# Sink-window attention with a Fourier mix: x transposes ahead of the probabilities' transposes, and three DVE instructions one step later

## The chip, the cores and the metric

The kernel runs on one core of one Trainium2 chip. The metric is the device time of one execution in microseconds (us); lower is better. The engines of the core are named as in the profile: PE is TensorE (PEld its weight loads), DVE is VectorE, ACT is ScalarE, POOL is GpSimd, SP is SyncE, which issues most DMAs.

## The reference

Attention over 4 batches, 8 heads, 768 positions and head width 64, where each query sees the first 4 keys (the sink) and the 128 latest; then a 2-D Fourier transform of the result, of which the real part is added; then a normalization and a two-layer network.

```python
keep = is_sink | in_window            # pos < 4, or 0 <= pos_q - pos_k < 128
a = exp(where(keep, q @ k.T / 8, -1e9) - max)
x = (a / (sum(a) + 1e-9)) @ v         # (4, 8, 768, 64) -> (4, 768, 512)
u = x + real(fft(fft(x, axis=1), axis=2))
un = (u - mean(u)) / sqrt(var(u) + 1e-6)
out = u + max(un @ w_ch1, 0) @ w_ch2  # 512 -> 2048 -> 512
```

## The kernel before, in words

**Groups and steps.** A group g (0 to 23) is one block of 128 queries of one batch, with all 8 heads; six groups make a batch. A step s = 4g + k treats the head pair k of group g. At each step every engine gets its share of several groups, since each operation has a lag in steps: in `STEP_LAG` for operations of a head pair, in `BLOCK_AT` for operations of a whole group.

**One group's path.** Scores s (PE, L703); the newer keys merged in (DVE, L709) and mask with maximum (DVE, L721, called soft1); the exponential (ACT, L727); the transposes of four heads' probabilities into the PSUM tile pt (PE, L755), copied to SBUF as pta (ACT, L762); selects on POOL that make ptl and zero a part of pta (L771, L779); the products with v into xt (PE, L793), copied as xs (ACT, L798); four transposes of xs into x (PE, L805) and one product that adds the sink's share (L807). The sink's probabilities go through a transpose of their own, pk (PE, L811), copied as skt (ACT, L816). POOL adds 1e-9 to the sums (floor, L747), DVE inverts them (inverse, L743) and multiplies x by them into u (store_x, L821).

**The Fourier mix** starts for a batch when its fourth block of u is stored. Stage 1 (L395) makes five PSUM tiles in turn: za0, za1, zr, zb0, zb1. Each is rounded to a high half by ACT (L402, L400 for zr), and DVE subtracts that for the low half (L410, L407 for zr). Stage 2 makes dc and a (L422) and b (L443) for three column blocks; ACT copies a to asb (L431), DVE forms sum and difference (L448, L449; L457 puts in the constant row), and POOL adds them to u (L459, L460). Batches 0 to 2 have stage 1 within attention; batch 3, the tail, has it after attention, beside the network.

**What shares a PSUM bank.** pt and pk have one buffer together. x has one. Stage-1 and stage-2 tiles have the buffer "fft", and at steps with k = 2 (`X_AT`) outside of steps 81 to 97 (`X_NOT`) they take x's buffer: za1 and zb0 of batches 0 and 1 share x's bank, while all five z tiles of batch 2 follow each other in the one "fft" bank. The transposes unx (L545) of the normalized batch 0, read by DVE at L554, share x's bank as well. A PE write to a bank waits for the last read of what was there.

**What sets the order.** Up to step 96 the instructions stand on each engine in the order in which they are recorded, and each engine works through its own queue in order. The table `SCHEDULE` has two phases, of which the second counts from step 36 (`PHASE`); for each engine and each k it lists operations and events: A, G and T are the transform's events on ACT, POOL and PE, and 0 to 3 and V those on DVE. From step 97 (`CUT`) to the end a scheduler orders the instructions. The network is ch1 (L620), relu (L1114, L1119) and ch2 (L1126); its weights are unpacked by DVE (L591 to L593), rounded by ACT (L608), and POOL takes the remainder (L609).

Of the kernel before, what the change touches and what calls it, by code (L numbers as in the profile page):

```python
# [72 lines left out]
    "copy_sink": 10,  # L73
    "sink_hi": 0,
    "floor": 6,
    "inverse": 8,
    "store_x": 13,
    "sink_lo": 2,
    "trans_sink": 9,
# [48 lines left out]
            ["sink_p", "newer_p", "older_p", "G"],  # L128
        ],
        "T": [  # L130
            ["av", "trans_p", "trans_sink", "T", "turn_x"],
            ["T", "trans_sink"],
            ["av", "T", "trans_p", "trans_sink", "turn_x"],
            ["trans_p", "T", "av", "trans_sink", "turn_x"],
# [4 lines left out]
EV_D, EV_Z = 1, 1  # L139
# [67 lines left out]
def kernel(  # L207
# [15 lines left out]
    V, A, G, T = nc.vector, nc.scalar, nc.gpsimd, nc.tensor  # L223

    def f32(ap):
        return ap.bitcast(F32)
# [44 lines left out]
    def run(general):  # L271
        tag = "g" if general else ""
        with ExitStack() as p1:
# [8 lines left out]
            def at(s, eng, fn):  # L282
                ev.setdefault((s, eng), []).append(fn)
# [49 lines left out]
            def fourier(b, at, ready):  # L333
# [49 lines left out]
                def stage1(kind, mc, part, parts):  # L383
                    ps = t_[f"z{kind}{mc}"] if part else psum(f"z{kind}{mc}")
                    ch, cl = (C_hi, C_lo) if kind != "b" else (S_hi, S_lo)
                    lo_c = {"a": P * mc, "r": 256, "b": 257 if mc == 0 else 384}[kind]
                    cs = slice(lo_c, lo_c + P)
                    mm = []
                    for j in range(NHALF):
                        mm += [(gh[:, j, cs], ch[:, j]), (gh[:, j, cs], cl[:, j]), (gl[:, j, cs], ch[:, j])]  # L390
                    if kind != "b":
                        mm += [(sph[:, cs], sgn)]
                    for i, (a, c) in enumerate(mm):
                        if i * parts // len(mm) == part:
                            T.matmul(ps[:, :NK], a, c, start=i == 0, stop=i == len(mm) - 1)  # L395

                def z_hi(kind, mc):
                    ps = t_[f"z{kind}{mc}"]
                    if kind == "r":
                        A.copy(zr[0:1], ps[0:1, :NK])  # L400
                    else:
                        A.copy((za if kind == "a" else zb)[0][:, mc], ps[:, :NK])  # L402

                def z_lo(kind, mc):
                    ps = t_.pop(f"z{kind}{mc}")
                    if kind == "r":
                        V.tensor_tensor(zr[NR - 1:NR], ps[0:1, :NK], f32(zr[0:1]), op=ALU.subtract)  # L407
                    else:
                        z = za if kind == "a" else zb
                        V.tensor_tensor(z[1][:, mc], ps[:, :NK], f32(z[0][:, mc]), op=ALU.subtract)  # L410
# [53 lines left out]
                tail = b == B - 1 or general  # L464
                at(1, "S", load_row)
                for j in range(NHALF):
                    k = ready[j]
# [11 lines left out]
                k = ready[2] + S1  # L479
                n1, na, nb = PARTS_TAIL if tail else PARTS[b]  # L480
                for i, (kind, mc) in enumerate((("a", 0), ("a", 1), ("r", 0), ("b", 0), ("b", 1))):
                    n = n1[i]
                    for part in range(n):
                        at(k + part, "T", lambda kind=kind, mc=mc, part=part, n=n: stage1(kind, mc, part, n))
                    k += n
                    at(k, "A", lambda kind=kind, mc=mc: z_hi(kind, mc))
                    at(k, EV_Z, lambda kind=kind, mc=mc: z_lo(kind, mc))
                k += S2
                for part in range(na):
                    at(k + part, "T", lambda part=part: stage2a(0, "dc", part, na))  # L490
# [143 lines left out]
            hp = []  # L634

            def window_attention(fourier, load_constants):
                with ExitStack() as pa:
                    kpool = pa.enter_context(tc.tile_pool(name="kpool", bufs=1, side="right"))
# [190 lines left out]
                    with ExitStack() as man:  # L829
# [130 lines left out]
                        while s < last:  # L960
# [25 lines left out]
                            for e in "AVGT":  # L986
                                for op in SCHEDULE[s >= PHASE][e][k]:
                                    if op in EVENTS:
                                        if (s, op) == (4, "G"):
                                            load_constants()  # L990
                                        run_ev(s, op)
                                    elif op in STEP_LAG:
                                        lag(table[op], s, STEP_LAG[op])
                                    else:
                                        at_ = s - BLOCK_AT[op]
                                        if at_ % NP == 0 and 0 <= at_ // NP < NQ:
                                            table[op](at_ // NP)
                                            if op == "store_x" and at_ // NP % NB == 3:
                                                b = at_ // NP // NB
                                                fourier(b, lambda d, e, f, s=s: at(s + d, e, f), FOLD_AT if b < B - 1 else FOLD_LAST)  # L1000
                            s += 1
                    extra.clear()
                return last

            def general_attention(fourier):
                for b in range(B):
                    u = uview(b)
# [331 lines left out]
```

## Time and profile before

| | us |
|---|---|
| median of 3 runs | 782.7 (782.69 to 784.17) |
| profiled execution | 786.08 |
| its span | 784.1 |
| mean granted PE clock | 0.991 |
| DVE, ACT, POOL busy | 453.5, 237.1, 185.1 |

Read as follows: the attention with the Fourier mix of batches 0 to 2 fills the first 200 us or so, the mix of batch 3 and the first of the seven groups of the network run up to about 280, and the rest is the network. Step 36 begins near 62 us and step 97 near 199 us of the span. In a row of a timeline stand the start, the duration, the engine, the line, the operation, out<-in and the shape; in brackets the idle time of the engine before it and what ended it. In a row of waits stand the waiting instruction, what it waited for, and the total in us, the count and the longest.

### The profile page before, as it was taken

To read this page: it belongs to the slowest core of one execution; us is meant where nothing else is said; L and a number is where in the kernel's file an instruction comes from. 1 tells how busy PE (TensorE), PEld (TensorE's weight loads), DVE (VectorE), ACT (ScalarE), POOL (GpSimd) and SP (SyncE) were. 2 spreads that over 40 slices of the span, in tenths; PEclk is the share of its full clock that TensorE was granted. 3 is DMA by queue.
4 is the path that set the end of the run, shared out by engine and by line. 5 is a ranking of instruction groups with operands and counts; after the bars stand their busy time and mean duration, and the time that the engine had idled before them with its cause. 6 is when DMAs were issued, how large, how long until landed. Compare 5 with 4: busy or idle time off the path is not lost.

```text
span 784.1 us, 11917 instructions
## 1 busy us (share of the span) xinstructions
PE 755.7 (96%) x4379; PEld 616.8 (79%) x4379; DVE 453.5 (58%) x1330; ACT 237.1 (30%) x704; POOL 185.1 (24%) x307
## 2 busy tenths in 40 slices
PE   7999998989998999999999999999999999999996
PEld 5676876867777878899888888888888888888895
DVE  6878587999999489561456424661456424611211
ACT  4887765766523123221111101111111111110110
POOL 2567477477654255100000000000000000000000
PEclk9999999999999899999999999999999999999998
DMA  9863535434215266110100002000200001000100
GB/s 283 268 177 105 151 83 177 127 112 145 86 50 166 92 196 208 66 59 1 54 0 1 1 18 89 1 0 1 81 0 1 2 1 54 1 0 1 54 1 31
DMA packets 41810, 57.67 MB, mean 74 GB/s; under 512 B 2796, under 2 KB 27500, under 8 KB 41360
## 3 DMA queue, kind: packets, MB, share of 16 engines
q1 hardware_dynamic: 41456, 53.07, 21.6%
q0 software_dynamic: 288, 3.76, 1.3%
q8 instruction: 36, 0.59, 0.3%
q14 instruction: 30, 0.25, 0.1%
HBM read 47.37 MB, written 9.45 MB: 72 GB/s over the span
## 4 chain that ended last, share of the span: by engine, by line
PE 80%; DVE 9%; POOL 4%; issue 3%; ACT 2%; DMA 2%; SPq 1%; POOLq 0%; DVEq 0%; ACTq 0%
PE o L1126 33%; PE h L620 33%; PE s L703 3%; PE xt L793 3%; PE pt L755 2%; PE za L395 1%; DVE cv L592 1%; DVE cv L593 1%; DVE sm L721 1%; PE zb L395 1%; ACT pta L762 1%; ACT sm L727 1%; DMA vt<-in_v_sink_dram 1%; POOL ptl L771 1%; DVE s L709 1%
## 5 line engine op out<-in xcount | busy, mean ns | idle before, releaser
L1126 PE MATMUL o<-w,h 128*128 128x512 f32 x876 | 218.6, 397 | 0.0
L1119 DVE SCALAR_TENSOR_TENSOR h<-h,h 128x512 fp32r<-128x512 f32 (+1 forms) x107 | 65.4, 611 | 250.5 <-ACT h L1114 250.3
L1126 PEld LDWEIGHTS o<-w,h 128*128 128x128 f32 x876 | 164.5, 190 | 36.0
L1114 ACT ACTIVATE h<-h 128x512 fp32r<-128x512 f32 (+1 forms) x107 | 57.1, 534 | 368.6 <-PE h L620 362.4
L620 PE MATMUL h<-un_slots,w 128*128 128x512 f32 (+1 forms) x576 | 124.7, 365 | 0.0
L620 PEld LDWEIGHTS h<-un_slots,w 128*128 128x128 f32 x576 | 99.6, 188 | 19.6
L620 PE MATMUL h<-un_last,w 128*128 128x512 f32 (+1 forms) x432 | 89.0, 355 | 0.0
L620 PEld LDWEIGHTS h<-un_last,w 128*128 128x128 f32 x432 | 72.7, 188 | 12.8
L727 ACT ACTIVATE sm<-sm,mx 128x132 f32<-128x132 f32 x192 | 76.0, 400 | 6.0 <-DVE mx L721 6.0
L1150 DVE STREAM_TRANSPOSE unf<-un 32x128 f32<-32x128 f32 x224 | 67.7, 302 | 3.2
L703 PE MATMUL s<-ring,q 64*128 64x260 f32 x320 | 49.9, 418 | 8.9 <-DVE mx L721 5.3
L721 DVE CUSTOM_DVE_ANT_0 sm<-s,mask 128x132 f32<-128x132 f32 x192 | 48.5, 293 | 6.3 <-PE s L701 1.3
L703 PEld LDWEIGHTS s<-ring,q 64*128 64x128 f32 x320 | 27.3, 188 | 21.6 <-issue 8.0
L609 POOL TENSOR_TENSOR w<-cv,w 128x512 fp32r<-128x512 f32 x25 | 34.1, 1366 | 30.5 <-ACT w L608 30.5
L793 PE MATMUL xt<-ptl,ldv 128*64 128x128 f32 x384 | 39.3, 285 | 0.2 <-POOL ptl L771 0.2
L727 ACT ACTIVATION_READ_ACCUMULATOR sm<-sm,mx 128x1 f32 x192 | 36.7, 191 | 0.0
L1126 PE MATMUL o<-w_ring,h 128*128 128x512 f32 x144 | 35.6, 393 | 0.0
L762 ACT COPY pta<-pt 128x512 f32<-128x512 f32 x48 | 28.0, 583 | 24.9 <-PE pt L755 23.5
L709 DVE COPY_PREDICATED s<-older,s 128x256 f32<-128x256 uint8 x80 | 33.7, 421 | 1.6 <-PE s L703 1.6
L771 POOL TENSOR_SCALAR_AFFINE_SELECT ptl<-pta 128x512 f32<-128x512 f32 x48 | 32.5, 678 | 7.3 <-ACT pta L762 7.2
L793 PEld LDWEIGHTS xt<-ptl,ldv 128*64 128x64 f32 x384 | 21.9, 136 | 15.1 <-issue 6.2
L793 PE MATMUL xt<-pta,ldv 128*64 128x128 f32 x320 | 31.7, 274 | 0.3 <-POOL pta L779 0.3
(197 smaller groups left out, 1039.4 us busy)
## 6 DMA issues: line engine op xcount, KB each, us to landing
raw<-in_moe_w_ch_dram SPq DMA_DIRECT2D x32, 512.0 KB, 3.7
ldv<-in_v_dram SPq DMA_DIRECT2D x28, 256.0 KB, 3.3
ring<-in_qk_dram SPq DMA_DIRECT2D x24, 264.0 KB, 4.8
out_dram<-u SPq DMA_DIRECT2D x24, 256.0 KB, 2.1
q<-in_qk_dram SPq DMA_DIRECT2D x20, 256.0 KB, 4.4
cst<-in_dft_dram POOLq DMA_DIRECT2D x1, 3348.0 KB, 12.8
ud<-us SPq DMA_DIRECT2D x12, 256.0 KB, 2.1
u<-ud SPq DMA_DIRECT2D x2, 1024.0 KB, 4.9
```

Of the source, the lines that this page charges most:

```text
L620: T.matmul(ps[:, :tb], a[:, cs], x[:, :, cc, :], start=n == 0, stop=n == 3 * NCC - 1)
L703: T.matmul(ps[:, j, :P + W], st["q", g][rows, hp, :], keys(g, 2 * hp + j), start=True, stop=True)
L709: V.copy_predicated(ps[:, :, P + NS:P + W], older[qi > 2], ps[:, :, 0:P])
L721: V.tensor_tensor_reduce(sm[:, h % 4], ps[:, j, P:P + W], mask[min(qi, 3)], -SCALE, 3.0e38, ALU.add, ALU.min, accum_out=mx[:, 0, h:h + 1])
L727: A.activation(sm[:, h % 4], sm[:, h % 4], AF.Exp, bias=mx[:, 0, h:h + 1], scale=-1.0, accum_out=mx[:, 1, h:h + 1])
L762: A.copy(a, st.pop(("pt", g, hp // 2)))
L771: G.affine_select(lo, a, [[0, 4], [s, P]], compare_op=ALU.is_ge, fill=0.0, base=0, channel_multiplier=-s)
L793: T.matmul(ps[D * j:D * j + D, p, :], st["v", kb(g) - i][:, h, :], a[:, h % 4, :], start=i == 0, stop=i == n - 1)
L1114: A.activation(h[0], ps[:, :tb], AF.Relu)
L1119: V.scalar_tensor_tensor(h[1], ps[:, :tb], 0.0, f32(h[0]), op0=ALU.max, op1=ALU.subtract)
L1126: T.matmul(po[i], a[:, ts_], x, start=f == 0 and n == 0, stop=f == NF - 1 and n == 2)
L1150: V.transpose(unf[32 * q:32 * q + 32, :, r], un[r].rearrange("p (c q j) -> p c q j", c=NCC, q=4)[:, :, q])
```

## The change

Three edits, all in the order of work:

1. From step 36 on, at steps with k = 0, PE's list is `av, turn_x, trans_p, T` in place of `av, trans_p, trans_sink, T, turn_x`. So the x transposes (L805, L807) of groups 6 to 23 stand ahead of the pt transposes (L755) and ahead of the matmuls of the transform's event T of that step. (`trans_sink` does nothing at k = 0.)
2. `inverse` has lag 9 in place of 8: the reciprocal (L743) moves from a step with k = 0 to the next with k = 1, where it stands right ahead of `store_x`, for all groups.
3. The low halves of the first and the third stage-1 tile (za0 at L410, zr at L407) are recorded one step later, for batches 0 to 2.

```diff
-    "inverse": 8,
+    "inverse": 9,
...
         "T": [
-            ["av", "trans_p", "trans_sink", "T", "turn_x"],
+            ["av", "turn_x", "trans_p", "T"],
...
                     at(k, "A", lambda kind=kind, mc=mc: z_hi(kind, mc))
-                    at(k, EV_Z, lambda kind=kind, mc=mc: z_lo(kind, mc))
+
+                    at(k + (not tail and i in (0, 2)), EV_Z, lambda kind=kind, mc=mc: z_lo(kind, mc))
```

Lines behind the last edit have a number higher by one in the changed kernel (L806 is L805 of before).

On PE at group 6, the first one that the new list concerns: `pt_1` are the probabilities, `x_` the x transposes, `pk_` the sink's transpose. Before:

```order
L793 MATMUL xt_1046<-pta_1_960,ldv_803 64x128 x2
L755 MATMUL pt_1_1055<-ident,sm_0_936 128x128 x4
L805 MATMUL x_1060<-ident,xs_1006 128x128 x4
L807 MATMUL x_1060<-vs_722,skt_980 128x512
L811 MATMUL pk_1083<-ident_r,sk_917 128x128
L703 MATMUL s_2_1085<-ring,q_816 128x260 x2
```

And now:

```order
L794 MATMUL xt_1045<-pta_1_959,ldv_803 64x128 x2
L806 MATMUL x_1054<-ident,xs_1006 128x128 x4
L808 MATMUL x_1054<-vs_722,skt_980 128x512
L756 MATMUL pt_1_1060<-ident,sm_0_935 128x128 x4
L812 MATMUL pk_1083<-ident_r,sk_917 128x128
L704 MATMUL s_2_1085<-ring,q_816 128x260 x2
```

pt now stands directly ahead of pk, in whose bank it lies.

On PE in batch 2, where stage 1 makes zr (steps of group 22): before, the x transposes stand in the middle of zr's ten matmuls, behind pt:

```order
L755 MATMUL pt_1_2861<-ident,sm_0_2709 128x128 x4
L395 MATMUL zr_2_2866<-cst,gh_2210 128x386 x2
L395 MATMUL zr_2_2866<-cst,gl_2211 128x386
L395 MATMUL zr_2_2866<-cst,gh_2210 128x386 x2
L805 MATMUL x_2872<-ident,xs_2812 128x128 x4
L807 MATMUL x_2872<-vs_2159,skt_2770 128x512
L395 MATMUL zr_2_2866<-cst,gl_2211 128x386
```

And now ahead of all of it:

```order
L806 MATMUL x_2860<-ident,xs_2811 128x128 x4
L808 MATMUL x_2860<-vs_2159,skt_2770 128x512
L756 MATMUL pt_1_2866<-ident,sm_0_2708 128x128 x4
L395 MATMUL zr_2_2871<-cst,gh_2210 128x386 x2
L395 MATMUL zr_2_2871<-cst,gl_2211 128x386
L395 MATMUL zr_2_2871<-cst,gh_2210 128x386 x2
```

x moved up by nine instructions, and pt and zr down by five.

On DVE in batch 2, from the store of group 19 (`us_1`) to za1's low half; s_2 and s_3 are group 22's scores. Before:

```order
L821 TENSOR_TENSOR us_1_2618<-x_2736,mx_2297 128x512
L410 TENSOR_TENSOR za_2_2213<-za_2_2730,za_2_2212 128x386
L709 COPY_PREDICATED s_2_2764<-older_122,s_2_2764 128x2x128
L591 TENSOR_SCALAR cv_3108<-raw_3005 128x512
...
L709 COPY_PREDICATED s_3_2767<-older_122,s_3_2767 128x2x128
...
L743 RECIPROCAL mx_2574<-mx_2574 128x8
L593 SCALAR_TENSOR_TENSOR cv_3108<-raw_3005,cv_3108 128x512
L410 TENSOR_TENSOR za_2_2213<-za_2_2797,za_2_2212 128x386
```

And now:

```order
L822 TENSOR_TENSOR us_1_2618<-x_2724,mx_2296 128x512
L710 COPY_PREDICATED s_2_2764<-older_122,s_2_2764 128x2x128
...
L710 COPY_PREDICATED s_3_2767<-older_122,s_3_2767 128x2x128
L592 TENSOR_SCALAR cv_3108<-raw_3004 128x512
...
L410 TENSOR_TENSOR za_2_2213<-za_2_2735,za_2_2212 128x386
L457 COPY d_0_2648<-dcs_2327 1x514
L593 SCALAR_TENSOR_TENSOR cv_3108<-raw_3004,cv_3108 128x512
L594 SCALAR_TENSOR_TENSOR cv_3108<-raw_3004,cv_3108 128x512
L410 TENSOR_TENSOR za_2_2213<-za_2_2796,za_2_2212 128x386
```

za0's low half moved behind the merges and maxima of both score tiles, and the reciprocal went out of this stretch.

On DVE one group later, past step 97, around the store of group 20 (`us_0`); `mx_2433` before and `mx_2432` now belong to group 20, `mx_2710` and `mx_2709` to group 22. Before:

```order
L539 TENSOR_SCALAR un_3_2885<-u_64,stat_0_1899 128x512
L821 TENSOR_TENSOR us_0_2617<-x_2872,mx_2433 128x512
L407 TENSOR_TENSOR zr<-zr_2_2866,zr 1x386
L709 COPY_PREDICATED s_2_2897<-older_122,s_2_2897 128x2x128
...
L743 RECIPROCAL mx_2710<-mx_2710 128x8
```

And now:

```order
L540 TENSOR_SCALAR un_3_2884<-u_64,stat_0_1898 128x512
L744 RECIPROCAL mx_2573<-mx_2573 128x8
L822 TENSOR_TENSOR us_0_2617<-x_2860,mx_2432 128x512
L744 RECIPROCAL mx_2709<-mx_2709 128x8
L710 COPY_PREDICATED s_2_2897<-older_122,s_2_2897 128x2x128
...
L407 TENSOR_TENSOR zr<-zr_2_2871,zr 1x386
```

zr's low half moved behind the next scores' merges and maxima, and the reciprocal of group 22 moved up to where the low half was.

## The prediction

> **What bounds the kernel now.** I read the page first, then busy time by stage, then the idle time on VectorE (DVE) and TensorE (PE) where the edits lie.
>
> ```profile
> PE 755.7 (96%) x4379; PEld 616.8 (79%) x4379; DVE 453.5 (58%) x1330; ACT 237.1 (30%) x704; POOL 185.1 (24%) x307
> ```
>
> Over the whole span PE is the bound. The edits act only from step 36 (g6's x transposes, near 65 us) to the end of attention, so the stages there decide; the columns are PE, PEld, DVE, ACT and POOL busy, then the granted clock.
>
> ```profile
> 62.00:107.00 45.00, 43.47 (x391) 34.89 (x391) 30.26 (x135) 31.93 (x118) 26.56 (x57) 1.00 0.44 124
> 107.00:139.00 32.00, 29.11 (x244) 21.73 (x245) 26.92 (x99) 19.21 (x74) 23.10 (x42) 1.00 0.50 154
> 139.00:187.00 48.00, 44.17 (x399) 34.92 (x399) 46.19 (x173) 32.19 (x120) 34.89 (x62) 1.00 0.39 119
> 187.00:200.00 13.00, 13.00 (x115) 11.03 (x109) 10.96 (x39) 8.55 (x30) 8.33 (x17) 1.00 0.33 104
> 200.00:254.80 54.80, 49.01 (x297) 41.31 (x295) 54.32 (x89) 20.37 (x46) 31.57 (x27) 0.99 0.33 106
> 254.80:261.00 6.20, 6.16 (x18) 5.24 (x19) 0.69 (x1) 1.28 (x4) 1.28 (x1) 0.50 0.26 85
> 280.00:400.00 120.00, 120.00 (x627) 102.05 (x626) 67.59 (x137) 26.83 (x52) 20.89 (x17) 1.00 0.26 87
> ```
>
> From 62 to 107 PE is full (43.47 of 45), DVE is not: there a wait taken from DVE is worth nothing, and a wait given to PE costs its full length. From 139 to 254.8 DVE is full (46.19 of 48, 54.32 of 54.8, and 10.96 of 13 where batch 2's Fourier stage 1 runs): there DVE sets the pace and PE's 3.83 and 5.79 us of idle time are spare. From 280 to 400 PE never stops, with DVE at 67.59 of 120, and the work after that is of the same kind. So the end moves by as much as PE's return to work moves, and that hangs on one DVE instruction:
>
> ```profile
> 254.23 0.55 DVE L410 TENSOR_TENSOR zb<-zb,zb 128x386 fp32r<-128x386 f32 x1
> 254.84 1.66 PE L422 MATMUL a<-cst,za 128*128 128x258 f32 x6 [2.62 <-DVE zb L410]
> ```
>
> PE sat idle 2.62 us for it. What DVE loses or gains between 139 and 254 passes one for one into the end.
>
> **The change: early x transposes.** Nothing is added or removed; 18 groups of x rows go ahead of the probabilities' pt. x had been work between pt and whatever waits for pt's copy. At g6:
>
> ```profile
> 64.97 0.66 PE L755 MATMUL pt<-ident,sm 128*128 128x128 f32 x4
> 65.46 0.60 PE L805 MATMUL x<-ident,xs 128*128 128x128 f32 x4
> 66.30 0.28 PE L811 MATMUL pk<-ident_r,sk 128*128 128x128 f32 x1
> 65.66 0.59 ACT L762 COPY pta<-pt 128x512 f32<-128x512 f32 x1 [0.94 <-PE pt L755]
> PEld pk L811 <- ACT pta L762: 4.0, 9, 0.9
> ```
>
> pk uses pt's bank, so it needs the copy, which ended at 66.25; x hid that wait exactly. Now pt ends where x ended (66.30), the copy of 0.59 follows bare, and pk starts near 66.95: +0.65. The ends are 0 (if cover comes from elsewhere) and 0.9, the longest such wait so far. At g10 and g11 x stood between the last a matmul and b, which reads a's copy asb (one buffer, same bank):
>
> ```profile
> 99.97 0.29 PE L422 MATMUL a<-cst_row,zr 128*128 128x258 f32 x1
> 100.09 0.60 PE L805 MATMUL x<-ident,xs 128*128 128x128 f32 x4
> 100.76 0.95 PE L443 MATMUL b<-cst,zb 128*128 128x258 f32 x6
> 100.29 0.37 ACT L431 COPY asb<-a 128x257 f32<-128x257 f32 x1 [2.39 <-PE a L422]
> 160.12 0.63 PE L443 MATMUL b<-cst,zb 128*128 128x258 f32 x3 [1.01 <-ACT asb L431]
> ```
>
> The copy ends at 100.66, b starts at 100.76. With x ahead of a, b waits for 0.03 of latency, 0.37 of copy and some 0.1 behind: +0.5 (ends 0 and 1.0, the longest wait for asb, at 160.12). At g11 the same loss falls into 107 to 139, where PE has 2.89 us spare, and counts nothing. The other plain groups of the DVE-bound stretch cost nothing either. Sum of the early part: **+1.15 us**.
>
> **The change: low halves and reciprocal, batches 0 and 1.** In batch 0 (72 to 96 us) PE is full, so what DVE gains there is worth nothing. x shares a bank with za1 and zb0 there, and in the changed order asks for it where pt stands now:
>
> ```profile
> 79.98 0.56 DVE L410 TENSOR_TENSOR za<-za,za 128x386 fp32r<-128x386 f32 x1 [0.99 <-ACT za L402]
> 81.47 0.66 PE L755 MATMUL pt<-ident,sm 128*128 128x128 f32 x4
> 89.47 0.56 DVE L410 TENSOR_TENSOR zb<-zb,zb 128x386 fp32r<-128x386 f32 x1 [0.83 <-ACT zb L402]
> 90.52 0.66 PE L755 MATMUL pt<-ident,sm 128*128 128x128 f32 x4
> ```
>
> The low halves end at 80.54 and 90.03, 0.9 and 0.5 us before that, so nothing is lost either. In batch 1 two DVE waits go:
>
> ```profile
> 134.81 0.20 DVE L743 RECIPROCAL mx<-mx 128x8 f32<-128x8 f32 x1 [0.50 <-POOL mx L747]
> 134.55 0.48 ACT L402 CAST za<-za 128x386 fp32r<-128x386 f32 x1 [0.29 <-PE za L395]
> 138.79 0.69 DVE L821 TENSOR_TENSOR u<-x,mx 128x512 f32<-128x512 f32 x1 [0.57 <-PE x L807]
> 145.72 0.55 DVE L410 TENSOR_TENSOR zb<-zb,zb 128x386 fp32r<-128x386 f32 x1
> 145.60 0.66 PE L755 MATMUL pt<-ident,sm 128*128 128x128 f32 x4
> ```
>
> That is 1.07 us. Against it: za0's half now stands directly ahead of za1's, which still has to wait for ACT's cast to 135.03 (some 0.25); and x of g15, which shares zb0's bank, is now wanted where pt stood (145.60), while zb0's half ends at 146.27 and six more small statistics instructions (about 1.5 us) are placed ahead of it. PE then stalls 0.7 to 1.8 us, with pt and the next scores behind it in its queue. I take **+0.2** for the end (ends -1.1, all gained, and +1.0).
>
> **Batch 2, where most of it lies.** All five z tiles use one bank, so each stage-1 group waits for the low half of the one before.
>
> ```profile
> 182.32 0.66 PE L755 MATMUL pt<-ident,sm 128*128 128x128 f32 x4
> 182.40 0.68 DVE L554 TENSOR_TENSOR un_slots<-unx,un_slots 128x512 fp32r<-128x512 f32 x1
> 186.94 0.56 DVE L410 TENSOR_TENSOR za<-za,za 128x386 fp32r<-128x386 f32 x1 [0.41 <-ACT za L402]
> 187.90 0.59 PE L395 MATMUL za<-cst,gh 128*128 128x386 f32 x2
> 190.47 0.50 ACT L402 CAST za<-za 128x386 fp32r<-128x386 f32 x1
> 191.00 0.56 DVE L410 TENSOR_TENSOR za<-za,za 128x386 fp32r<-128x386 f32 x1
> 194.62 0.69 DVE L821 TENSOR_TENSOR us<-x,mx 128x512 f32<-128x512 f32 x1 [0.22 <-PE x L807]
> 196.99 0.55 DVE L407 TENSOR_TENSOR zr<-zr,zr 1x386 fp32r<-1x386 f32 x1 [1.68 <-ACT zr L400]
> 197.96 0.60 PE L395 MATMUL zb<-cst,gh 128*128 128x386 f32 x2
> 196.48 0.24 POOL L747 TENSOR_SCALAR mx<-mx 128x8 f32<-128x8 f32 x1
> ```
>
> Removed on DVE: 0.41 + 0.22 + 1.68 = 2.31 us. Added:
> 1. x of g19 is wanted at 182.32, where pt stood, but its bank is also that of unx, which DVE reads until 183.08: PE 0.8 late, DVE about 0.35 at the store.
> 2. za0's half now stands behind the four mask-and-maximum pairs of g22, so it ends near 189.1 instead of 187.4. za1 wants the bank at 187.9: PE stalls about 1.25. Everything on PE is late by this: ACT's za1 cast and DVE's second L410 go from 191.0 to about 192.5, with DVE idle some 1.6.
> 3. The reciprocal of g22 now comes right behind the store of g20. It waits for POOL's floor L747, which ended at 196.72 and follows pt's copy and two selects: pt is 0.67 later behind x, and PE 1.2 later by 2, so the floor ends near 198.6. The store ended at 195.2 and is itself later by about 1: DVE idles 2.3. So the 1.68 at zr comes back as a wait for POOL.
> 4. zr's half is behind the eight instructions that follow; zb0 wants its bank at about 199.5 and gets it near 201: PE stalls about 1.45 with pt and the xt products queued behind. DVE has conversions to do there, so I charge nothing more.
>
> Added: 0.35 + 1.6 + 2.3 = 4.25, less 2.31: **+1.95**, rounded 2.0. Ends: -2.3 (all removed waits pass, nothing comes back) and +4.0 (PE's stalls of 3 and 4 reach DVE too).
>
> **Sum.** 1.15 + 0.2 + 2.0 = +3.35. The profiled execution took 786.08 us for its span of 784.1; the change would make it 789.4. The median shown is 782.7, so I predict 782.7 + 3.4 = **786.1**. The gap of 2.62 and the half clock behind it stay, 3.4 later.
>
> **A row and a rule on the clock.**
>
> ```profile
> 107.33 0.93 PE L703 MATMUL s<-ring,q 64*128 64x260 f32 x6 [1.24 <-DMA ldv<-in_v_dram]
> ```
>
> PE's clock fell to 0.50 after the gap of 2.62 us and stayed so until 261: 6.2 us of work that would take 3.1. The gap of 1.24 us at 107 left it at 1.00. The added stalls, 1.25 to 1.45 each, lie just above the harmless one. The Trainium skill, TensorE: Matmul & The Clock Gate, section Part 1: The HAM clock gate (the "warmup" mystery), says that the clock halves after at least one idle window of about 3.4 us. By that rule no stall here would cost more than itself, and the sum stays; the 2.62 us row disagrees with it, since a shorter gap sufficed, so a rival below keeps the price.
>
> **Rivals.**
> - *The clock drops at a new stall* (0.10): two PE stalls of batch 2 run together, past 1.24 us towards 2.62. One half-clock stretch costs up to 3.1 us in a stretch where PE has little spare: 786.1 + 1.7 to 3.1, about 788.5.
> - *Nothing measurable* (0.17): PE's idle time from 107 on (2.89, 3.83 and 5.79) takes in the early 1.15 and the stalls, and DVE's added waits equal the 3.4 removed. Then 782.7 to 784.2, about 783.3. For it: the groups after 200 have spare PE time; against: DVE has almost none.
> - *The removed DVE waits arrive* (0.13), the other side: the low halves leave the banks before PE asks for them, so terms 2 and 3 vanish. It decides at za1: if za0's half ends by 187.9 and the floor by the time of the reciprocal, DVE arrives 1.07 + 2.31 = 3.4 earlier at 254. That gives 779.3; if the gap then shrinks below what drops the clock, another 3.1: 776.2. Against it: DVE's queue is in order, and the moved half has about 1.7 us of g22's work ahead of it.
> - *The change does not do what it says*: excluded for the order, which is shown above; but if the moved halves carried no one's wait, it would be the second rival.
>
> **Chances.** Forecast 0.60, clock drop 0.10, nothing 0.17, gain 0.13. A measurement can tell about 0.2% (1.6 us) from no change; slower takes the forecast and the drop, with a little of the forecast's low end given to same: faster 0.13, same 0.19, slower 0.68. The forecast's own range is 784.3 to 788.5. For 8 in 10 I go from 780.0, inside the gain, to 789.5, above most of the clock drop.
>
> **What would show it.** Right: in the changed profile pk of g6 waits about 0.65 for pta; b of g10 about 0.5 for asb; PE waits over 1 us for L410 at za1 and for L407 at zb0 of batch 2; DVE waits some 2 us for POOL's floor at the reciprocal; and the matmul behind the 2.62 gap starts near 258.2 instead of 254.84. Wrong: if it starts earlier than 254.8, the removed waits did pass; if it starts later by 3.4 but the end does not, PE had spare work after 255 that these rows do not show.

## The result and the profile after

The changed kernel takes 792.06 us (median of 4 runs, 791.3 to 795.75) against 783.43 of before in the same comparison: a ratio of 1.0118, interval 1.0083 to 1.0154. A second comparison, change_again below, gives 1.0094 (1.0080 to 1.0107), 792.2 against 784.16. So the change costs some 8 us: the direction was forecast, the size was not (3.4), and the time lies outside the range.

The stages of the changed kernel, as in the prediction's table but with a cut at 160 (PE, PEld, DVE, ACT and POOL busy, then the granted clock):

```profile
62.00:107.00 45.00, 43.19 (x391) 35.06 (x391) 28.95 (x129) 31.07 (x117) 25.22 (x55) 1.00 0.42 119
131.00:160.00 29.00, 26.92 (x243) 21.73 (x239) 25.14 (x114) 18.02 (x70) 14.15 (x32) 1.00 0.43 125
160.00:187.00 27.00, 22.38 (x201) 16.85 (x200) 23.99 (x80) 16.48 (x61) 21.31 (x36) 1.00 0.34 101
187.00:200.00 13.00, 12.29 (x101) 10.30 (x100) 10.99 (x44) 7.28 (x27) 8.80 (x15) 1.00 0.54 177
200.00:254.80 54.80, 47.92 (x308) 40.52 (x307) 50.52 (x89) 21.94 (x57) 30.70 (x32) 0.97 0.26 79
254.80:261.00 6.20, 6.20 (x30) 5.26 (x30) 6.17 (x8) 2.21 (x5) 4.03 (x3) 1.00 0.62 189
```

DVE, which had been full from 139 to 254.8, now is not: 23.99 of 27, 50.52 of 54.8. It has not got more to do, it waits. Where PE and DVE wait in the changed kernel (idle time before the instruction, and what ended it, in brackets):

```profile
66.59 0.28 PE L812 MATMUL pk<-ident_r,sk 128*128 128x128 f32 x1 [0.67 <-ACT pta L763]
101.19 0.99 PE L443 MATMUL b<-cst,zb 128*128 128x258 f32 x6 [0.46 <-ACT asb L431]
148.32 0.66 PE L806 MATMUL x<-ident,xs 128*128 128x128 f32 x4 [1.44 <-DVE zb L410]
171.74 0.44 PE L546 MATMUL unx<-ident,un 128*128 128x128 f32 x2 [1.38 <-DVE u L822]
193.16 0.62 PE L395 MATMUL za<-cst,gh 128*128 128x386 f32 x2 [0.71 <-DVE za L410]
205.76 0.84 PE L422 MATMUL a<-cst,za 128*128 128x258 f32 x5 [2.26 <-DVE mx L722]
236.75 0.44 PE L395 MATMUL za<-cst,gh 128*128 128x386 f32 x1 [2.49 <-ACT gh L365]
262.79 0.88 PE L422 MATMUL a<-cst,za 128*128 128x258 f32 x5 [0.85 <-DVE zb L410]
152.78 0.56 DVE L410 TENSOR_TENSOR zb<-zb,zb 128x386 fp32r<-128x386 f32 x1 [1.46 <-ACT zb L402]
164.32 0.42 DVE L448 TENSOR_TENSOR d<-asb,b 128x257 f32<-128x257 f32 x1 [2.23 <-PE b L443]
196.28 0.56 DVE L410 TENSOR_TENSOR za<-za,za 128x386 fp32r<-128x386 f32 x1 [1.19 <-ACT za L402]
202.70 0.20 DVE L744 RECIPROCAL mx<-mx 128x8 f32<-128x8 f32 x1 [2.25 <-POOL mx L748]
221.75 0.69 DVE L822 TENSOR_TENSOR us<-x,mx 128x512 f32<-128x512 f32 x1 [1.69 <-PE x L808]
```

pk, b, x at zb0's bank, za1's cast and the reciprocal wait about as forecast. Not forecast are the DVE waits at 152.78, 164.32 and 221.75 (5.4 us together) and the PE waits at 171.74, 205.76 and 236.75. The instruction of before's 254.84, the first a matmul of batch 3, now starts at 262.79: 7.95 later, not 3.4. But its gap shrank from 2.62 to 0.85 and no half clock follows it, where before had 6.2 us of it in its row. So the span of this execution is longer by 5.2 only (789.3 against 784.1). A shorter stretch at half clock lies earlier instead; it is why the row from 200 says 0.97. The stretch behind the a matmul, then the earlier one:

```profile
262.79:266.20 3.41, 3.41 (x18) 2.98 (x19) 0.69 (x1) 1.25 (x4) 1.29 (x1) 1.00 0.49 154
218.50:221.91 3.41, 3.41 (x17) 2.75 (x16) 1.72 (x5) 0.62 (x1) 2.64 (x2) 0.50 0.29 74
```

### The profile page after: what moved, and what is told of

Read it like the earlier page. It is cut to its first block, busy times and chain, and to the rows that moved or that the text cites. A ratio compares the mean times of both kernels' runs of the same rounds, so it can differ in the third digit from the quotient of the medians.

```text
span 789.3 us, 11916 instructions
## 1 busy us (share of the span) xinstructions
PE 754.9 (96%) x4379; PEld 617.3 (78%) x4379; DVE 452.2 (57%) x1330; ACT 236.9 (30%) x704; POOL 185.1 (23%) x307
## 4 chain that ended last, share of the span: by engine, by line
PE 77%; DVE 12%; POOL 3%; issue 3%; DMA 2%; ACT 1%; SPq 1%; DVEq 0%; POOLq 0%; ACTq 0%
PE o L1127 32%; PE h L621 32%; PE xt L794 3%; PE s L704 3%; PE pt L756 2%; DVE cv L593 1%; DVE sm L722 1%; PE za L395 1%; DVE s L710 1%; DVE cv L592 1%; DVE cv L594 1%; PE x L806 1%; DMA ring<-in_qk_dram 1%; DMA vt<-in_v_sink_dram 1%; PE zb L395 1%
## 5 line engine op out<-in xcount | busy, mean ns | idle before, releaser
L722 DVE CUSTOM_DVE_ANT_0 sm<-s,mask 128x132 f32<-128x132 f32 x192 | 48.5, 293 | 9.6 <-PE s L702 3.3
```

The lines of the kernel that those rows point to most:

```text
L722: V.tensor_tensor_reduce(sm[:, h % 4], ps[:, j, P:P + W], mask[min(qi, 3)], -SCALE, 3.0e38, ALU.add, ALU.min, accum_out=mx[:, 0, h:h + 1])
```

## The experiments

Each compares a kernel with before on one chip. Ratios are to before, with their 95% intervals. The three edits stand alone or in pairs:

```diff
 x_only:  SCHEDULE[1]["T"][0] = ["av", "turn_x", "trans_p", "T"]
 i_only:  "inverse": 9
 z_only:  at(k + (not tail and i in (0, 2)), EV_Z, ...)
 x_z:     x_only and z_only, "inverse": 8
```

**x_only.** 

> Only the first edit: x transposes ahead of the pt transposes from step 36; low halves and reciprocal as before. Theory A (the waits that the edits put on shared banks add up in the stretch where DVE is the bound, each edit with its own share): the early waits of pk and b (0.67 and 0.46 in the changed kernel), the wait of x for zb0's low half in batch 1 (1.44), and the two DVE waits behind it (1.46 and 2.23 in the changed kernel) come with this edit alone, those of za1 (1.19) and of the reciprocal (2.25) do not: about 787.5, +4. Theory B (no edit costs much alone; the scheduler's new order past step 97, which only the three edits together bring about, costs the time): within 1.6 of before, 782 to 785.

791.02, ratio 1.0070 (1.0055 to 1.0085): most of the cost comes with the first edit. Theory A stands, with a larger share than it gave; theory B falls. The trace has the waits that A named. DVE's are of nearly the same length as in the full change; x's at zb0's bank is 0.75 against 1.44 there:

```profile
147.89 0.66 PE L805 MATMUL x<-ident,xs 128*128 128x128 f32 x4 [0.75 <-DVE zb L410]
152.35 0.56 DVE L410 TENSOR_TENSOR zb<-zb,zb 128x386 fp32r<-128x386 f32 x1 [1.58 <-ACT zb L402]
163.88 0.42 DVE L448 TENSOR_TENSOR d<-asb,b 128x257 f32<-128x257 f32 x1 [2.12 <-PE b L443]
```

**z_only.** 

> Only the third edit: low halves of za0 and zr one step later, all else as before. Theory A: DVE waits 1.2 for za1 and PE waits for zr's low half at zb0, while the 1.68 that DVE waited at zr goes: +0.5 to +2, 784 to 785.5. Theory B: within 1.6 of before, 782 to 785. An earlier thought of mine, that the moved halves pay by themselves: -1 to -2, 781.5 to 782.5.

785.2, ratio 1.0008 (0.9993 to 1.0023): nothing that can be measured. Its interval fits A as well as B; the earlier thought of a gain of 1 to 2 falls. It loses and gains: PE waits for za0's half and at zb0, but the wait at the first a matmul of batch 3 is 0.74 where before had 2.62.

```profile
188.32 0.62 PE L395 MATMUL za<-cst,gh 128*128 128x386 f32 x2 [0.98 <-DVE za L410]
205.62 0.62 PE L395 MATMUL zb<-cst,gh 128*128 128x386 f32 x2 [1.80 <-DVE zb L410]
255.93 0.99 PE L422 MATMUL a<-cst,za 128*128 128x258 f32 x6 [0.74 <-DVE zb L410]
```

**i_only.** 

> Only the second edit: the reciprocal one step later. Theory A: the 0.5 at the reciprocal of batch 1 goes; past step 97 the reciprocal of group 22 waits some 1.5 for the floor, in place of the 1.68 at zr: -0.5 to +0.5, 783 to 784. Theory B: within 1.6 of before, 782 to 785. If it is the reciprocal by itself that costs (its wait of 2.25 in the changed kernel): +2, 785.5.

785.26, ratio 1.0011 (0.9996 to 1.0025): no difference, and its interval tells none of the three expectations from the others. In its trace the reciprocal of group 22 waits 1.45 for the floor, as expected.

**x_z.** 

> The change without the second edit: the reciprocal as before, so that no reciprocal waits for the floor behind the store of group 20. Theory A: the sum of the two single edits, 788.5 to 790.5, less than the change's 792.1 by what the reciprocal's wait costs (0 to 2.25). Theory B: 784 to 786, since one of the three is missing.

788.03, ratio 1.0036 (1.0022 to 1.0051): just under A's range and above B's. It is less than x_only, so the first and third edit do not add. The third, with no cost that can be measured alone, takes 0.34% off the first; and the second adds some 0.6% to the two (change_again against x_z, run beside other runs of before).

**change_again.** 

> The whole change once more, for comparison on one chip. 790.5 to 793 by every theory; in PE's idle time a wait of about 2.3 at the first a matmul of batch 2 past step 97, and DVE about 2.2 at the reciprocal of group 22.

792.2, ratio 1.0094 (1.0080 to 1.0107), with the waits of 2.25 at both places.

**late_recip_back**, the whole change but for

```diff
-    at_ = s - BLOCK_AT[op]
+    at_ = s - (8 if op == "inverse" and s >= 96 else BLOCK_AT[op])
```

> The whole change, but the reciprocals of groups 22 and 23 at their old lag of 8. Theory C (the second edit costs only through the reciprocal of group 22, which waits for POOL's floor behind the store of group 20 and holds up DVE's soft1, zr's low half and the a matmuls of PE behind them): the time of the change without the second edit, 788 to 789.5, no DVE wait for the floor at that place. Theory D (the reciprocal's other moves, in attention, or the pure accident of the scheduler's order cost the rest): 791 to 792.5, as the whole change.

789.02, ratio 1.0061 (1.0049 to 1.0074): 0.33% under the change on the same chip. Theory C: one reciprocal carries 2.6 us. The edit moves that of group 23 back too, but this one waits in neither trace. DVE waits at another place, and less; PE's wait of 2.26 at the a matmul fell to 0.33, and that for gh from 2.49 to 0.60:

```profile
202.29 0.43 DVE L710 COPY_PREDICATED s<-older,s 128x256 f32<-128x256 uint8 x1 [1.05 <-PE s L704]
204.63 0.84 PE L422 MATMUL a<-cst,za 128*128 128x258 f32 x5 [0.33 <-DVE mx L722]
232.77 0.61 PE L395 MATMUL za<-cst,gh 128*128 128x386 f32 x2 [0.60 <-ACT gh L365]
260.38 0.99 PE L422 MATMUL a<-cst,za 128*128 128x258 f32 x6 [1.34 <-DVE zb L410]
```

Whether the rest, against x_z, is the second edit's other moves is open: the intervals 1.0049 to 1.0074 and 1.0022 to 1.0051 just touch, and the two were run against other runs of before.

**x_i**, the first and second edit. 

> The first and second edit, low halves as before. Theory C: the reciprocal of group 22 waits for the floor here too, which x ahead of pt has made later, but zr's low half, next behind it, would have waited for ACT by 2.0 anyway (x alone), so it costs 0 to 1 on top of x alone: 790.5 to 792. If the second edit costs the same wherever the first is: 794 to 795 (x alone and the 4 us that the second adds to the first and third).

791.69, ratio 1.0088 (1.0075 to 1.0102): as theory C says.

**z_i**, the second and third. 

> The second and third edit, x transposes as before. Theory A': the first edit is what costs, since PE's stalls come with it; pt and so the floor are not later here, and the reciprocal waits some 1.5 at most: 784.5 to 786.5. If the second and third edit together cost without the first: 788 to 789.

786.7, ratio 1.0031 (1.0020 to 1.0042), just above theory A': without the first edit the two cost 2.5 us together. Neither is clear of zero alone, but the sum of their two ratios, 0.19%, is not told from 0.31% by these intervals.

**Where the first edit costs.** The new list is used in a range of steps only (the kernel is else that of before):

```diff
-    for op in SCHEDULE[s >= PHASE][e][k]:
+    for op in (EARLY_X if e == "T" and k == 0 and 36 <= s < 64 else SCHEDULE[s >= PHASE][e][k]):
```

and so with `64 <= s < 88`, `s >= 88`, and `s >= 36 and s not in (72, 88)`.

**x_36_63.** 

> The first edit alone, and only in steps 36 to 63 (groups 6 to 12, up to about 130 us). Theory E (PE is full from 62 to 107 and again from 131 to 160, so each wait that the new order gives to PE ahead of 160 costs its length, and DVE's later waits only show it): pk of group 6 waits 0.67, b of group 10 0.46, b of group 11 and pk of group 12 0.3 net: +1.1 to +1.6 on before, 785.3 to 786. Theory P (as predicted, DVE sets the pace from 139 and PE's idle time there is spare): the same 1.15, or less where the spare time takes it in: 784 to 785.3.

785.6, ratio 1.0009 (0.9997 to 1.0021), about +0.7 us, which tells neither theory from the other; the waits are there (pk 0.68 at 66.11 and at 121.97).

**x_64_87.** 

> The first edit alone, and only in steps 64 to 87 (groups 13 to 18, about 130 to 182 us). Theory E: the wait of x of group 15 for zb0's low half, the dc copy and the wait of b for asb come in PE's full stretch and behind it: +2 to +3, 786 to 787. Theory P: 0.2, with ends -1.1 and +1.0: 783 to 785.

786.78, ratio 1.0032 (1.0019 to 1.0044), +2.5 us: theory E, and theory P is out by its upper end. It holds the whole chain of batch 1:

```profile
146.22 0.66 PE L806 MATMUL x<-ident,xs 128*128 128x128 f32 x4 [0.74 <-DVE zb L411]
156.23 0.75 PE L423 MATMUL a<-cst,za 128*128 128x258 f32 x4 [0.45 <-ACT dcs L427]
161.14 0.98 PE L444 MATMUL b<-cst,zb 128*128 128x258 f32 x6 [1.01 <-ACT asb L432]
150.68 0.56 DVE L411 TENSOR_TENSOR zb<-zb,zb 128x386 fp32r<-128x386 f32 x1 [1.59 <-ACT zb L403]
162.23 0.42 DVE L449 TENSOR_TENSOR d<-asb,b 128x257 f32<-128x257 f32 x1 [2.12 <-PE b L444]
```

x waits for zb0's low half; dc and b are late behind it on PE (b's wait of 1.01 itself stood in before too, at 160.12); DVE, which had no wait at either place before, then waits 1.59 and 2.12 for what PE and ACT deliver late.

**x_88_on.** 

> The first edit alone, and only from step 88 on (groups 19 to 23, and another order past step 97). Theory E: x of group 19 waits for unx's low half (1.0), ptl and xt are late past 200 (1.2): +1 to +2.2, 785 to 786.4. Theory P: +0.35 at the store, less what is gained at the store of group 20: 784 to 785. If most of the cost of the first edit were the scheduler's order past step 97: +4 or more, 788.

786.49, ratio 1.0037 (1.0022 to 1.0051), +2.9 us, above theory E's 1 to 2.2 and below the 4 of the last clause. The waits that E named are there, and a third that it did not name, at the store of group 22:

```profile
182.40 0.66 PE L806 MATMUL x<-ident,xs 128*128 128x128 f32 x4 [0.73 <-DVE un_slots L555]
202.60 0.44 PE L794 MATMUL xt<-ptl,ldv 128*64 128x128 f32 x4 [1.20 <-POOL ptl L772]
209.83 0.44 PE L794 MATMUL xt<-ptl,ldv 128*64 128x128 f32 x4 [1.53 <-POOL ptl L772]
215.63 0.69 DVE L822 TENSOR_TENSOR us<-x,mx 128x512 f32<-128x512 f32 x1 [2.15 <-PE x L808]
```

The three ranges add up to 0.78%, against 0.70% of x_only.

**x_not_72_88.** 

> The first edit alone, but with the old order at steps 72 and 88, the two where x is asked for while its bank is still read (zb0's low half of batch 1; unx's low half). Theory E: x alone less 0.75 and 1.03 of PE's wait: 788 to 789.5. Theory F (these two bank waits carry most of it, with DVE's waits of 1.58 and 2.12 as their echo): 785.5 to 787.5.

787.35, ratio 1.0042 (1.0029 to 1.0055): at theory F's upper end, under E's range. Two steps out of 18 carry some 0.28%, 2.2 us; but not all, and the DVE wait of 2.12 at the combine stays, so that one is not an echo of the bank waits alone.

**The two halves of the third edit**, `i == 2` (zr) or `i == 0` (za0) in place of `i in (0, 2)`, on top of the first edit, and zr's without it.

**x_zr.** 

> The first edit with zr's half of the third only. Theory G (of the third edit, za0's late half costs, as PE waits 0.71 at za1; zr's late half gains, since with it the scheduler puts other work ahead of the wait for L410 at 255 to 262 us, and PE's gap there falls from 2.6 to about 1.3, with no half clock behind it): less than first and third together, 786.5 to 788, PE's gap at the first a matmul of batch 3 about 1.3. Theory H (both halves of the third edit gain a bit each): 789 to 790, between the first edit alone and with the third.

787.48, ratio 1.0035 (1.0019 to 1.0050).

**x_za.** 

> The first edit with za0's half of the third only. Theory G: no less than the first edit alone, 790.5 to 792, PE's gap at the first a matmul of batch 3 about 2.6. Theory H: 789 to 790.

790.91, ratio 1.0082 (1.0059 to 1.0105). So it is zr's late half that takes 0.35%, some 2.7 us, off the first edit (1.0070 to 1.0035), and za0's that gains nothing, as theory G says; x_zr is 3.4 us under x_za beside the same runs of before. But the way that G gave is wrong: the gap at the first a matmul of batch 3 is 1.30 with zr's and 1.52 with za0's half, no great difference. In x_za PE waits for ptl twice as x_only does, and for za0; in x_zr these waits are smaller or gone:

```profile
193.27 0.62 PE L395 MATMUL za<-cst,gh 128*128 128x386 f32 x2 [0.72 <-DVE za L410]
207.87 0.44 PE L793 MATMUL xt<-ptl,ldv 128*64 128x128 f32 x4 [1.21 <-POOL ptl L771]
215.10 0.44 PE L793 MATMUL xt<-ptl,ldv 128*64 128x128 f32 x4 [1.54 <-POOL ptl L771]
```

In x_zr the same stretch shows:

```profile
208.33 0.44 PE L793 MATMUL xt<-pta,ldv 128*64 128x128 f32 x4 [0.55 <-POOL pta L779]
210.89 0.66 PE L805 MATMUL x<-ident,xs 128*128 128x128 f32 x4 [1.02 <-DVE un_slots L554]
214.70 0.44 PE L793 MATMUL xt<-pta,ldv 128*64 128x128 f32 x4 [0.47 <-POOL pta L779]
```

That is 3.47 us of waits against 2.04, so it accounts for 1.4 of the 3.4. The remaining 2 us are not placed.

**zr_only.** 

> zr's half of the third edit alone: a version that may beat both. Theory G: the third edit alone (785.2) without the wait of PE for za0's half (1.3 from 187 to 200 us): 782.5 to 784, faster than before by 0 to 1.7; PE's gap at the first a matmul of batch 3 below 1.4. Theory H: 784 to 785.5, as before.

783.54, ratio 0.9986 (0.9970 to 1.0002): the only kernel below before, at the value of theory G, but its interval reaches no change. Its gap at the first a matmul of batch 3 is 1.10. Nothing here is shown to beat before.

## Why the prediction missed: point by point

- **The step that failed** is the reading of the bound: "From 139 to 254.8 DVE is full ... there DVE sets the pace and PE's 3.83 and 5.79 us of idle time are spare." The stage was cut too coarsely. Cut at 160, before reads

```profile
131.00:160.00 29.00, 28.00 (x260) 23.03 (x258) 26.93 (x118) 19.47 (x74) 17.15 (x38) 1.00 0.48 135
160.00:187.00 27.00, 24.17 (x210) 18.77 (x212) 25.92 (x84) 17.05 (x64) 22.83 (x37) 1.00 0.39 127
```

  and PE's one idle microsecond of the first row is the wait of 1.01 that ends at 160.12. Up to there PE was at least as full as DVE (28.00 against 26.93 of 29); nearly all of the 3.83 lay behind. So the stall of x at zb0's bank, forecast at 0.7 to 1.8 and measured at 0.74 (first edit alone) to 1.44, was not spare time: it made zb1, dc, b and the scores late, and DVE waited for ACT's cast of zb1 and for b (1.46 and 2.23) with nothing to catch up in. Batch 1 was priced at +0.2; steps 64 to 87 of the first edit alone cost 2.5. The prediction's row from 187 to 200 says against it too: PE 13.00 of 13, DVE 10.96. In z_only, which has the third edit alone, pt's copy of 183.01 in before starts at 182.19, and the next one, of 189.51, at 189.95: between them, with PE's wait of 0.98 at za1, the work fell behind by 1.26, so PE had nothing to spare there either. (That z_only ends no later is read beside its gap at batch 3, 0.74 instead of 2.62.)
- **The reciprocal of group 22**: the wait was forecast at 2.3 and measured at 2.25. The price was wrong. I set the 1.68 at zr against it and charged "nothing more" for what stands behind. late_recip_back shows 2.6 us for this one instruction: behind it on DVE stands soft1 of group 23, whose end frees the bank of the a matmuls that the scheduler had put ahead of zb0 on PE. In term 4 I had PE wait 1.45 for zr's half at zb0; it waited 2.26 one place earlier, for L722, and the waits for gh and x followed. That PE's wait hangs on the reciprocal is shown by late_recip_back, where it is 0.33.
- **Early part**: pk 0.65 forecast, 0.67 measured; b 0.5 and 0.46. Sum 1.15 against about 0.7 of x_36_63, inside its interval. Right for these two. The loss at group 11, counted as nothing since PE had 2.89 us spare from 107 to 139, was not nothing in the trace: pt's copy of 105.44 in before starts 0.47 later in the changed kernel, that of 114.36 starts 1.19 later. Batch 0: no PE gap between 67 and 101 in the changed kernel. Right.
- **Batch 2**: PE at za1 1.25 forecast and 0.71 measured; DVE there 1.6 and 1.19; x of group 19 0.8 and 0.42 (0.73 in x_88_on). The waits were named rightly; the sum 2.0 was too small, since steps from 88 on cost 2.9 with the first edit alone and the reciprocal 2.6 on top, while zr's late half gave some 2.7 back, which I had not seen.
- **"The gap of 2.62 and the half clock behind it stay"**: it shrank to 0.85, and the clock behind it stayed at 1.00 (the row from 262.79). This hid part of the loss in the span of the profiled execution.
- **Rivals.** The gain was excluded by the result, and so was "nothing". The clock drop at new stalls did happen: 3.41 us at 0.50 from 218.5 in the profiled execution, worth 1.7 us. But before's had 6.2 us of it, so it does not make the difference. Nor does it over all executions: in the comparison of change_again the mean granted clock is 0.995 with the change and 0.996 before, by an estimate (0.001 of 790 us) worth under 1 us of the 8. The rival took the length of a gap, past 1.24 us towards 2.62, for what decides; the rows of x_36_63, x_64_87 and x_zr below show that it does not.

## What to carry to other kernels

Before idle time is called spare, cut the stage until each piece has either idle time or none: two engines can both be full in the first half of a window in which only one looks full, and there a stall of either is passed on to the other and comes back. Ask of a wait not only what it replaces, but which bank is freed by the instructions queued behind it, and which engine has that bank at the head of its queue. And edits that move the same instructions need not add: measured alone, the third costs nothing that can be told from noise, and one half of it takes half of the first edit's cost away.

## What was not expected of the hardware

The half clock after a gap on PE does not follow from the gap's length. Two kernels had a wait of 2.62 us at the first a matmul of batch 3: the row of the timeline and the window behind it, first of x_36_63:

```profile
258.29 0.39 PE L423 MATMUL a<-cst,za 128*128 128x258 f32 x1 [2.62 <-DVE zb L411]
```

```profile
258.29:261.70 3.41, 3.41 (x18) 2.97 (x19) 0.69 (x1) 1.25 (x4) 1.30 (x1) 1.00 0.45 154
```

Then of x_64_87:

```profile
256.48 0.39 PE L423 MATMUL a<-cst,za 128*128 128x258 f32 x1 [2.62 <-DVE zb L411]
```

```profile
257.00:260.41 3.41, 3.41 (x12) 2.85 (x12) 0.69 (x1) 0.72 (x3) 0.97 (x1) 0.50 0.41 145
```

The first ran on at full clock, the second had 3.4 us at half (18 matmuls against 12 in equal time), and before's profiled execution had 6.2 in its row of the prediction. What differs is how the gap lies to a grid. In each trace the half-clock stretches start whole multiples of 3.413 us apart (in x_not_72_88 at 111.85 and 238.15, 37 of them). In x_64_87 nearly the whole gap falls into one window of this grid, right ahead of the half clock:

```profile
253.59:257.00 3.41, 0.79 (x7) 0.59 (x6) 2.83 (x4) 1.75 (x4) 1.69 (x2) 1.00 0.57 162
```

In x_36_63 the grid, laid through its half-clock stretch at 109.74, cuts the gap in two:

```profile
109.74:113.15 3.41, 3.41 (x20) 2.90 (x18) 2.91 (x13) 0.00 (x0) 0.42 (x1) 0.50 0.00 0
253.10:256.51 3.41, 2.58 (x15) 2.09 (x13) 3.34 (x5) 1.32 (x3) 2.06 (x2) 1.00 0.56 172
256.51:259.92 3.41, 1.63 (x10) 1.51 (x11) 2.42 (x4) 1.74 (x4) 2.01 (x2) 1.00 0.61 219
```

A gap of only 1.31 was followed by half clock in x_zr (row, the grid's window with the gap, and the stretch behind):

```profile
171.11 0.73 PE L545 MATMUL unx<-ident,un 128*128 128x128 f32 x3 [1.31 <-DVE u L821]
167.93:171.35 3.42, 1.92 (x18) 0.96 (x15) 3.42 (x9) 2.55 (x13) 2.94 (x7) 1.00 0.51 152
171.30:174.71 3.41, 3.25 (x16) 2.88 (x16) 2.69 (x14) 0.48 (x1) 1.75 (x5) 0.51 0.21 75
```

Cut so, by the grid through each trace's own half-clock stretches and from 10 to 766 us of all 17, half clock followed every full-clock window in which PE was busy for under 1.6 us and none in which it was busy for over 2.0; between the two it followed some (1.92 here) and not others (1.63 in x_36_63). What decides there is open.

The Trainium skill, TensorE: Matmul & The Clock Gate, section Part 1: The HAM clock gate (the "warmup" mystery), has windows of 3413 ns that run freely. The stretches of 3.4 us and the grid agree with that length, and where the grid lies differs from run to run, so whether a given gap costs the clock is luck. Its condition of at least one idle window does not agree, if idle means without work: windows with PE busy for 0.79 and 1.92 us were enough. Each such stretch costs about 1.7 us by an estimate (half of 3.41), as much as several of the differences studied here, so a single profiled span is no measure of an edit of this size.
